# A linear-attention and MLP block on one core: tile 3 of x loaded ahead of the keys' weight, tile 0 worked in halves, and the orders and banks laid out anew

## The chip, the core and the metric

The kernel runs on one core of one Trainium2 chip. The core has a matrix engine (TensorE, "PE" in the profile, its weight loads "PEld"), a vector engine (VectorE, "DVE"), a scalar engine (ScalarE, "ACT"), GpSimd ("POOL") and a sync engine ("SP") that here only issues DMA transfers. Each engine runs its own list of instructions in order and waits for others by semaphores. Matmuls write to the eight banks of PSUM, of 512 float columns each; everything else lies in SBUF. The metric is the device time of one execution in microseconds, the median over several runs.

## What is computed

One transformer block in bfloat16: x has 2048 rows of 512; there are 32 heads of 16, and the MLP is 1792 wide.

```python
def _A_ref(x, wqkv, wo):                       # linear attention
    q, k, v = split(x @ wqkv)
    phi = lambda t: jnp.where(t > 0, t + 1, jnp.exp(t)) + 1e-6
    pq, pk = phi(q), phi(k)
    kv = jnp.einsum("bhsd,bhse->bhde", pk, v)
    z = jnp.einsum("bhsd->bhd", pk)
    o = (pq @ kv) / (pq @ z + 1e-6)
    return o @ wo
...
h = x + _A_ref(_layernorm(x), A_wqkv, A_wo)
h2 = h + _B_ref(_layernorm(h), B_w1, B_w2)     # relu(h' @ w1) @ w2
```

The sum over all rows in kv and z splits the program: all keys come first, then the heads' matrix, and only then the rows of h.

## The kernel before

The 2048 rows are 16 tiles of 128 (t = 0 to 15) and 4 chunks of 512 (c = 0 to 3; tiles 4c to 4c + 3). Nothing is scheduled by a planner at build time: a table of words, `ORDER` (line 18), is read from left to right, and each word calls a small function (`op_` and its name, lines 181 to 563) that issues a few instructions with the numbers behind the points. So each engine's list is the table's order, filtered by engine; a word's place against words of other engines means nothing except through data. Semaphores between engines are set by the framework from what is written and read. The numbers of a word say the tile or chunk, often a PSUM bank, and a first column block and a count where the work is split.

The words that matter, with the line of their instruction:

- `lx.t.n` (219), `lk`, `lq`, `lv`, `lo`, `l1`, `l2` (225): loads of n tiles of x, and of the weights; all on SP.
- `S`, `A` (253, 254): statistics of a tile of x on DVE; `R` (259, 260): one over the standard deviation on ACT; `N` (267): the normalised tile on DVE. Small letters `s`, `a`, `r`, `n` (255, 256, 259, 275) do the same for h; `n` leaves the scale out, and `r` is applied in the last step.
- `T.t.b` (292): four transposes of a normalised tile on TensorE into bank b; `E` (302): ACT's copy of them to lnT. `X` and `x` (313, 314) do both in one DMA transpose, issued by SP; `x.t` reads hn, which `n.t` writes.
- `K.t.b.k.n` (321): n of the four key matmuls of a tile; `F`, `U`, `M`, `D` make the map phi of it. `Q` and `qF` to `qD` are the same for the queries.
- `G`, `z`, `kv`, `m`, `d4`, `wb`, `rb`, `ab`, `dm`: the heads' matrices and the denominators.
- `h.t.b` (501): attention output of a tile on TensorE, `hD` (507) the sum with x on DVE.
- `p.c.f.b` (516), `ph` (525, half the columns): block f of the MLP's first layer for chunk c, 4 matmuls that read the chunk's lnT, all 512 columns of it; `pD` (536, DVE) and `pA` (531, ACT): relu of one or two blocks.
- `f.t.b.f0.n` (545): n of the 14 matmuls of the second layer for a tile; `fo` (553): the last sum on DVE; `fd` (560): the store on SP, in full or, as `fd.t.0.2` and `fd.t.2.2`, in halves of 256 columns.

```python
def op_p(c, f, b):
    for kd in range(KD):
        nc.tensor.matmul(bk[:, b, :], lhsT=w1_sb[:, kd, f * P : (f + 1) * P], rhs=lnT[c][:, kd, :], ...)
op_x = lambda t: nc.sync.dma_start_transpose(out=lnT_of(t), in_=hn[:, t % NQ, :])
op_fd = lambda t, k=0, w=KD: store(nc.sync, t, k, w)
```

The buffers lnT of chunks 0 to 3 are used twice, first for x's rows, then for h's. hn holds eight tiles, o_t (named gT in the profile) four. SP issues its transfers strictly in the table's order: a transfer whose data are not ready holds up all behind it.

Of the kernel before, what the change touches and what calls it, by code (L numbers as in the profile page):

```python
# [15 lines left out]


ORDER = """
table const lx.0.1 warm.66.7.64 lx.1.1 masks lx.2.1 lk.0.4 lx.3.1 S.0 lx.4.2 S.1 lx.6.2 lq.0.4 A.0 A.1 S.2 R.0.1
warm.2.7 lx.8.4 R.1.1 N.0 lx.12.4 A.2 N.1 T.0.1 R.2.1 T.1.6 E.0 N.2 E.1 T.2.4 S.3 K.0.2 E.2 A.3 S.4 K.1.4.2.2 R.3.1  # L20
K.1.4.0.2 F.0.1 N.3 A.4 U.0.1 S.5 T.3.5 K.2.6.2.2 E.3 S.7 K.2.6.0.2 F.1.1 K.3.3.0.2 M.0.1 A.5 U.1.1 D.0.1 K.3.3.2.2
M.1.1 R.4.2 Q.0.3.1 S.6 F.3.1 A.7 A.6 N.5 F.2.1 Q.0.1.5 N.4 X.5 R.6.2 D.1.1 T.4.7 U.3.1 M.2.1 Q.0.0.4 M.3.1 S.8 E.4
lo.0.2 U.2.1 S.10 Q.0.2.0 qF.0.0.2 N.6 K.4.2 N.7 X.6 A.10 A.8 qU.0.0.2 S.9 K.5.3 D.3.1 X.7 A.9 D.2.1 R.8.2 G.0 S.15
F.4.2 N.8 G.1 S.13 X.8 U.4.2 S.14 G.3 qU.0.2.2 A.13 S.12 lv.0.2 G.2 M.4.2 A.12 N.9 K.7.3 R.12.2 A.15 D.4.2 X.9
qF.0.2.2 K.6.2 N.12 A.14 S.11 R.14.2 X.12 K.8.0 F.6.2 N.15 N.14 G.4 A.11 N.13 U.6.2 M.6.2 X.13 qM.0.0.2 K.9.1 R.10.2
qD.0.0.2 K.12.2 X.15 D.6.2 U.8.2 za.4.1 G.5 F.8.2 X.14 K.13.3 N.11 N.10 za.6.0 G.6 X.11 U.12.2 G.7 M.8.2 F.12.2 X.10
qM.0.2.2 K.14.0 D.8.2 M.12.2 K.15.1 lv.2.2 za.8.0 l1.0.2 K.11.3 l1.2.2 F.14.2 D.12.2 K.10.2 zf U.14.2 qD.0.2.2 G.9 zhi
F.10.2 M.14.2 G.13 zlo U.10.2 G.8 M.10.2 D.14.2 G.12 D.10.2 z.0.0 z.2.0 z.3.0 z.1.0 G.15 zc zh d4.0.2 G.11 dl4.0 dx4.0
G.14 wb.0 G.10 lo.2.2 Q.1.1.1 gA.2.2 gD.0.2 rb.0.4 Q.1.0.0 ab.0.1 rb.0.6 ab.0.3 kv.1.7 rb.0.2 kv.3.7 ab.0.7 kv.0.7
rb.0.0 kv.2.7 ab.0.5 Q.1.3.3 l2.7.7 kx qF.1.0.2 Q.1.2.2 qU.1.0.2 qM.1.0.2 m.0.4 m.2.6 m.1.5 qF.1.2.2 qD.1.0.2 m.3.7  # L30
Q.2.0.0 mD.0.2 mA.2.2 Q.2.1.1 qU.1.2.2 dm.0.0.2 Q.2.3.7 dm.0.2.2 qF.2.0.2 h.1.6 qM.1.2.2 qD.1.2.2 qU.2.0.2 h.0.2 hD.1
d4.1.4 s.1 Q.3.1.5 a.1 hD.0 nA.1 h.3.0 s.0 dl4.1 x.1 h.2.2 a.0 hD.3 nA.0 Q.2.2.6 s.3 dx4.1 x.0 Q.3.2.0 a.3 hD.2
qF.2.2.2 n.3 wb.1 Q.3.3.1 s.2 qU.2.2.2 x.3 Q.3.0.4 a.2 n.2 qF.3.2.2 qM.2.0.2 x.2 qM.2.2.2 ph.0.3.3.0 qU.3.2.2 qD.2.2.2
ph.0.0.6.0 ph.0.1.7.0 qM.3.2.2 rb.1.7 qU.3.0.2 ph.0.2.2.0 qD.3.2.2 rb.1.3 ph.0.11.1.0 rb.1.5 qD.2.0.2 ph.0.10.0.0
qF.3.0.2 rb.1.6 ph.0.10.0.1 rb.1.1 ph.0.11.1.1 rb.1.0 p.0.5.4 pD.0.10.2 rb.1.4 rb.1.2 ph.0.2.2.1 ph.0.3.3.1 l2.0.7
qM.3.0.2 ph.0.0.6.1 pD.0.2.2 p.0.6.0 ph.0.1.7.1 qD.3.0.2 p.0.4.3 pD.0.0.2 p.0.7.1 pA.0.4.2 dm.1.2.2 d4.2.5.2 dm.1.0.2
p.0.8.2 dl4.2 pD.0.6.2 dl4.3 p.0.9.3 dx4.2 p.0.13.5 dx4.3 pD.0.8.2 wb.2 r.0.4 h.4.7 h.6.0 hD.4 rb.2.3 f.3.1.0.7 rb.2.1
s.4 rb.2.0 a.4 rb.2.6 rb.2.2 p.0.12.4 rb.2.5 rb.2.7 h.7.2 pD.0.12.2 rb.2.4 f.3.1.7.7 wb.3 hD.7 s.7 h.5.4 hD.6
f.2.3.7.7 hD.5 f.1.6.0.7 dm.2.2.2 dm.2.0.2 s.6 rb.3.2 h.8.0 rb.3.7 a.6 s.5 f.1.6.7.7 rb.3.0 hD.8 rb.3.5 rb.3.6 n.4 s.8
rb.3.3 f.2.3.0.7 a.5 rb.3.1 fo.1 rb.3.4 n.5 a.7 x.5 h.9.7 n.7 n.6 fo.2 f.0.0.7.7 x.4 fo.3 dm.3.2.2 h.10.5 x.7 dm.3.0.2  # L40
h.11.6 hD.9 x.6 hD.10 h.13.3 s.10 h.15.2 fd.3.0.2 fd.3.2.2 a.10 a.8 n.10 hD.11 h.14.7 x.10 s.11 f.0.0.0.7 n.8 a.11
hD.15 s.9 p.1.3.5 hD.13 p.1.8.2 hD.14 fo.0 p.1.2.4 s.15 h.12.1 s.14 p.1.9.3 s.13 a.13 p.1.7.7 pD.1.8.2 p.1.6.6 a.9
n.11 r.8.4 n.13 p.1.12.0 n.9 r.4.4 a.14 a.15 x.9 n.14 p.1.11.3 hD.12 pD.1.2.2 p.1.13.1 x.11 p.1.10.2 n.15 pD.1.6.2 x.8
p.1.0.5 pD.1.10.2 p.1.5.4 fd.1.0.2 fd.1.2.2 x.14 p.1.1.6 s.12 pD.1.12.2 f.5.2.7.7 fd.2.0.2 fd.2.2.2 fd.0.0.2 fd.0.2.2
x.15 pD.1.0.2 p.1.4.3 p.2.2.5 pD.1.4.2 f.5.2.0.7 p.2.6.3 fo.5 p.2.7.4 p.2.3.6 pD.2.6.2 p.2.10.1 a.12 n.12 r.12.4
p.2.4.4 pD.2.2.2 x.12 f.7.0.0.7 fd.5.0.2 fd.5.2.2 x.13 f.7.0.7.7 p.2.5.5 fo.7 p.2.11.2 pD.2.4.2 p.2.12.3 pD.2.10.2
p.2.13.4 f.4.6.0.7 pD.2.12.2 p.2.0.5 p.3.2.1 p.3.3.2 f.4.6.7.7 f.6.0.0.7 fo.4 pD.3.2.2 p.3.9.7 p.3.8.6 f.6.0.7.7
pD.3.8.2 p.2.9.1 fo.6 p.2.1.6 fd.6 p.3.1.3 p.3.0.2 p.2.8.0 pD.3.0.2 p.3.11.4 pD.2.0.2 p.3.10.3 pD.2.8.2 p.3.5.2
p.3.6.6 pD.3.10.2 p.3.7.7 p.3.4.1 pD.3.6.2 f.8.3.0.7 pD.3.4.2 p.3.13.7 f.10.5.0.7 p.3.12.6 f.10.5.7.7 pD.3.12.2
f.14.4.0.7 fo.10 fd.10 fd.7 f.15.1.0.14.3.1 f.15.6.0.14.0.2 fo.15.3.1 fd.15.3.1 f.14.4.7.7 fd.4 f.8.3.7.7 f.13.0.0.7  # L50
f.9.7.0.7 f.13.0.7.7 f.11.5.7.7 fo.13 fo.15.0.2 fo.14 fd.15.0.2 f.11.5.0.7 fd.13 fo.8 fd.8 f.9.7.7.7 fo.11 f.12.1.0.7
fo.9 fd.9 fd.11 f.12.1.7.7 fd.14 f.15.2.0.14.2.1 fo.12 fd.12 fo.15.2.1 ad.15.2.1
"""


# [543 lines left out]
```

## Time and profile before

| | |
|---|---|
| median of 3 runs | 168.77 us (168.57 to 169.34) |
| profiled execution | 168.48 us |
| its span (first to last instruction) | 166.8 us |
| DVE / ACT busy | 115.9 / 49.5 us |
| DMA | 16.28 MB, 98 GB/s on average |

The span is what the profile's rows cover; the execution's time has 1.7 us around it. In the rows, "L516" is a line of the kernel, "out<-in" are the tiles written and read, "xN" the number of instructions in a merged row, and a bracket tells how long the engine had been idle before and what ended that. Matmuls are pipelined, so a row's duration is longer than the distance to the next. DMA issues ("SPq") show the time that the queue spends on issuing; the time to landing is told apart.

### The profile page before, as it was taken

Reading aid. Unit: us, or ns where it says so; the run is one execution under the profiler, and the core shown is the slowest. Engines: PE = TensorE matmul, PEld = TensorE weight load, DVE = VectorE, ACT = ScalarE, POOL = GpSimd, SP = SyncE. Lnnn points to the kernel's source line nnn. Section 1 sums busy time; section 2 is a strip of 40 time slices with the busy share of each in tenths; the row PEclk is TensorE's granted clock in tenths of the full one; section 3 lists DMA queues with packets and bytes.
Section 4 is the critical chain, followed back from the end, with each engine's and each line's share of the span. In section 5 each row is a group of like instructions: output and inputs, shape, how many; then the busy total and the mean of one; then the engine's idle time right before and its main releaser. Section 6 shows DMA issues by size and latency. Waiting matters only on the chain.

```text
span 166.8 us, 2421 instructions
## 1 busy us (share of the span) xinstructions
PE 162.6 (98%) x920; PEld 79.8 (48%) x920; DVE 115.9 (69%) x215; ACT 49.5 (30%) x83; POOL 4.8 (3%) x21
## 2 busy tenths in 40 slices
...
GB/s 113 346 300 126 125 97 103 276 253 96 170 177 51 111 135 210 72 94 56 111 109 69 0 63 93 100 30 64 0 0 4 31 0 0 7 97 2 44 95 73
DMA packets 26811, 16.28 MB, mean 98 GB/s; under 512 B 16176, under 2 KB 25776, under 8 KB 26800
## 3 DMA queue, kind: packets, MB, share of 16 engines
...
q10 hardware_dynamic: 464, 0.30, 0.7%
q8 instruction: 7, 0.11, 0.3%
q14 instruction: 4, 0.03, 0.1%
...
## 4 chain that ended last, share of the span: by engine, by line
PE 94%; DVE 2%; DMA 1%; ACT 0%; issue 0%
PE bk L545 29%; PE bk L516 26%; PE bk L321 8%; PE bk L373 8%; PE bk L329 8%; PE bk L501 8%; PE bk L525 3%; DMA x_nat<-in_A_x_dram 1%; DVE st L253 1%; PE bk L445 1%; DVE gT L553 1%; PE bk L397 1%; PE bk L292 1%; PE bk L419 1%; PE bk L431 1%; DVE h_nat L267 0%
## 5 line engine op out<-in xcount | busy, mean ns | idle before, releaser
L545 PE MATMUL bk<-w_sb,at 128*128 128x512 bf16 (+2 forms) x252 | 50.9, 355 | 0.0
L516 PE MATMUL bk<-lnT,w_sb 128*128 128x512 bf16 x200 | 45.6, 379 | 0.0
L536 DVE TENSOR_SCALAR at<-bk 128x1024 bf16<-128x1024 f32 x27 | 32.4, 1220 | 13.6 <-PE bk L516 10.6
L545 PEld LDWEIGHTS <-at 128*128 128x128 bf16 x252 | 23.5, 98 | 25.2 <-DVE at L536 0.3
L516 PEld LDWEIGHTS <-w_sb 128*128 128x128 bf16 x200 | 19.5, 98 | 23.1 <-issue 0.4
L553 DVE SCALAR_TENSOR_TENSOR gT<-bk,rstd,h_nat 128x512 bf16<-128x512 f32 (+2 forms) x18 | 12.1, 688 | 22.6 <-PE bk L545 20.2
L339 ACT ACTIVATE eb<-bk 128x1024 bf16<-128x1024 f32 (+1 forms) x18 | 16.6, 930 | 3.5 <-PE bk L419 1.6
L259 ACT ACTIVATE rstd<-mv,eps 128x2 f32<-128x2 f32 (+2 forms) x14 | 4.1, 294 | 44.4 <-DVE mv L256 41.6
L342 ACT ACTIVATE rb<-bk 128x1024 bf16<-128x1024 f32 (+1 forms) x18 | 16.6, 936 | 0.9 <-PE bk L321 0.9
L501 PE MATMUL bk<-m_sb,pqs 128*128 128x512 bf16 x64 | 15.3, 379 | 0.0
L321 PE MATMUL bk<-wk_sb,lnT 128*128 128x512 bf16 x64 | 15.1, 379 | 0.0
L329 PE MATMUL bk<-lnT,wq_sb 128*128 128x512 bf16 x64 | 15.0, 379 | 0.0
L373 PE MATMUL bk<-at,h_nat 128*128 128x512 bf16 x56 | 13.2, 379 | 0.0
L253 DVE BATCH_NORM_STATS2 st<-x_nat 128x6 f32<-128x512 bf16 x16 | 10.5, 675 | 1.9 <-DMA x_nat<-in_A_x_dram 1.9
L507 DVE TENSOR_TENSOR h_nat<-bk,x_nat 128x512 bf16<-128x512 f32 x16 | 10.7, 679 | 0.9 <-PE bk L501 0.8
L255 DVE BATCH_NORM_STATS2 st<-h_nat 128x6 f32<-128x512 bf16 x16 | 10.8, 687 | 0.2
L501 PEld LDWEIGHTS <-pqs 128*128 128x128 bf16 x64 | 6.3, 98 | 7.6
L373 PEld LDWEIGHTS <-h_nat 128*128 128x128 bf16 x64 | 6.1, 98 | 7.3 <-issue 0.2
L321 PEld LDWEIGHTS <-lnT 128*128 128x128 bf16 x64 | 6.0, 97 | 7.4 <-ACT lnT L302 0.3
L329 PEld LDWEIGHTS <-wq_sb 128*128 128x128 bf16 x64 | 6.1, 98 | 7.1 <-issue 0.2
L346 DVE TENSOR_SCALAR eb<-eb 128x1024 bf16<-128x1024 bf16 (+1 forms) x18 | 6.7, 389 | 0.3 <-ACT eb L339 0.3
L267 DVE TENSOR_SCALAR h_nat<-x_nat,mv,rstd 128x512 bf16<-128x512 bf16 x16 | 6.1, 400 | 0.3 <-ACT rstd L260 0.3
...
## 6 DMA issues: line engine op xcount, KB each, us to landing
...
x_nat<-in_A_x_dram SPq DMA_DIRECT2D x2, 512.0 KB, 7.1
...
wk_sb<-in_A_wqkv_dram SPq DMA_DIRECT2D x1, 512.0 KB, 4.2
...
```

What stands on the lines that cost most here:

```text
L253: op_S = lambda t: nc.vector.bn_stats(out=st[:, t, :], in_=x_nat[:, t, :])
L255: op_s = lambda t: nc.vector.bn_stats(out=st2[:, t, :], in_=h_nat[:, t, :])
L321: nc.tensor.matmul(bk[:, b, :], lhsT=lnT[c][:, kd, j * P : (j + 1) * P], rhs=wk_sb[:, kd, :], **part(("k", t), KD),)
L329: nc.tensor.matmul(bk[:, b, :], lhsT=wq_sb[:, kd, j * P : (j + 1) * P], rhs=lnT[c][:, kd, :], start=(kd == 0), stop=(kd == KD - 1),)
L339: nc.scalar.activation(out=buf(eb, kind, i, n), in_=bank(at_bank[kind, i], n), func=ACT.Exp)
L342: nc.scalar.activation(out=buf(rb, kind, i, n), in_=bank(at_bank[kind, i], n), func=ACT.Relu)
L373: nc.tensor.matmul(bk[:, KD + kd, :], lhsT=ln_nat[:, t, kd * P : (kd + 1) * P], rhs=pk(t)[:, 0, :], start=(not stated), stop=(len(stated) ...
L501: nc.tensor.matmul(bk[:, b, :], lhsT=pqs[:, (c * KD + jb) % NQ, j * P : (j + 1) * P], rhs=m_sb[:, jb, :], start=(jb == 0), stop=(jb == KD ...
L516: nc.tensor.matmul(bk[:, b, :], lhsT=w1_sb[:, kd, f * P : (f + 1) * P], rhs=lnT[c][:, kd, :], start=(kd == 0), stop=(kd == KD - 1),)
L536: nc.vector.tensor_scalar(out=acts[c % 2][:, f : f + n, :], in0=bank(at_bank["p", c, f], n), scalar1=-1.0, scalar2=0.0, op0=ALU.mult, op1= ...
L545: nc.tensor.matmul(bk[:, b, 0 : w * P], lhsT=acts[c % 2][:, f, j * P : (j + 1) * P], rhs=w2_sb[:, f, k * P : (k + w) * P], **part(("f", t, ...
L553: nc.vector.scalar_tensor_tensor(out=o_t[:, t % NO, cols], in0=bk[:, at_bank["f", t, k], 0 : w * P], scalar=rstd2[:, t : t + 1], in1=h_nat ...
```

## The change

Only the table changes. The first words now load tile 3 of x (`lx.3.1`) ahead of the keys' weight (`lk.0.4`). Tile 0's `N.0`, `T.0.1` and `E.0` become two each, first for columns 256 to 511, then for 0 to 255. All other words are the same in number and work, but nearly all of the table stands in a new order, with other banks. The table is a line longer, so every line of the code behind it has a number that is one higher.

```diff
-table const lx.0.1 warm.66.7.64 lx.1.1 masks lx.2.1 lk.0.4 lx.3.1 S.0 lx.4.2 S.1 lx.6.2 lq.0.4 A.0 A.1 S.2 R.0.1
-warm.2.7 lx.8.4 R.1.1 N.0 lx.12.4 A.2 N.1 T.0.1 R.2.1 T.1.6 E.0 N.2 E.1 T.2.4 S.3 K.0.2 E.2 A.3 S.4 K.1.4.2.2 R.3.1
-K.1.4.0.2 F.0.1 N.3 A.4 U.0.1 S.5 T.3.5 K.2.6.2.2 E.3 S.7 K.2.6.0.2 F.1.1 K.3.3.0.2 M.0.1 A.5 U.1.1 D.0.1 K.3.3.2.2
...
-h.11.6 hD.9 x.6 hD.10 h.13.3 s.10 h.15.2 fd.3.0.2 fd.3.2.2 a.10 a.8 n.10 hD.11 h.14.7 x.10 s.11 f.0.0.0.7 n.8 a.11
-hD.15 s.9 p.1.3.5 hD.13 p.1.8.2 hD.14 fo.0 p.1.2.4 s.15 h.12.1 s.14 p.1.9.3 s.13 a.13 p.1.7.7 pD.1.8.2 p.1.6.6 a.9
-n.11 r.8.4 n.13 p.1.12.0 n.9 r.4.4 a.14 a.15 x.9 n.14 p.1.11.3 hD.12 pD.1.2.2 p.1.13.1 x.11 p.1.10.2 n.15 pD.1.6.2 x.8
-p.1.0.5 pD.1.10.2 p.1.5.4 fd.1.0.2 fd.1.2.2 x.14 p.1.1.6 s.12 pD.1.12.2 f.5.2.7.7 fd.2.0.2 fd.2.2.2 fd.0.0.2 fd.0.2.2
-x.15 pD.1.0.2 p.1.4.3 p.2.2.5 pD.1.4.2 f.5.2.0.7 p.2.6.3 fo.5 p.2.7.4 p.2.3.6 pD.2.6.2 p.2.10.1 a.12 n.12 r.12.4
...
-fo.9 fd.9 fd.11 f.12.1.7.7 fd.14 f.15.2.0.14.2.1 fo.12 fd.12 fo.15.2.1 ad.15.2.1
+table const lx.0.1 warm.66.7.64 lx.1.1 masks lx.2.1 lx.3.1 lk.0.4 S.0 lx.4.2 S.1 lx.6.2 lq.0.4 A.0 A.1 S.2 R.0.1
+warm.2.7 lx.8.4 R.1.1 N.0.2.2 lx.12.4 A.2 N.0.0.2 T.0.2.2.2 R.2.1 N.1 T.0.6.0.2 E.0.2.2 T.1.5 N.2 E.0.0.2 S.3 E.1
+T.2.2 E.2 K.0.4 A.3 R.3.1 S.4 K.1.7.2.2 F.0.1 N.3 K.2.2.0.2 U.0.1 S.5 T.3.6 K.2.2.2.2 E.3 A.4 A.5 S.7 K.1.7.0.2 R.4.2
...
+pD.1.12.2 p.1.7.7 pD.1.8.2 p.1.1.4 a.9 p.1.4.1 a.13 a.15 pD.1.6.2 h.14.5 s.10 p.1.2.6 s.12 p.1.0.3 p.1.5.2 pD.1.0.2
+p.1.3.7 a.12 n.12 f.5.4.7.7 n.9 hD.14 x.9 a.10 n.15 pD.1.2.2 f.4.0.7.7 s.8 s.11 f.6.3.7.7 a.8 pD.1.4.2 f.4.0.0.7 n.10
+a.11 x.10 n.11 r.8.4 s.14 r.4.4 f.7.7.0.7 n.13 a.14 n.8 r.12.4 n.14 x.8 f.6.3.0.7 fd.0.0.2 fd.0.2.2 fd.1.0.2 fd.1.2.2
+fd.2.0.2 fd.2.2.2 f.5.4.0.7 x.11 f.7.7.7.7 x.13 fo.5 fd.5.0.2 fd.5.2.2 p.2.7.5 x.12 fo.7 fo.6 p.2.13.2 x.14 fo.4
...
+fo.9 fd.9 fd.14 f.15.0.0.14.2.1 fo.12 fd.12 fo.15.2.1 ad.15.2.1
```

How the lists of two engines move, at the places that the prediction speaks of. First SP at the start of the program; before:

```order
L219 DMA x_nat<-in_A_x_dram 128x512 x3
L225 DMA wk_sb<-in_A_wqkv_dram 128x4x512
L219 DMA x_nat<-in_A_x_dram 128x512
L219 DMA x_nat<-in_A_x_dram 128x1024 x2
L225 DMA wq_sb<-in_A_wqkv_dram 128x4x512
```

and now:

```order
L220 DMA x_nat<-in_A_x_dram 128x512 x4
L226 DMA wk_sb<-in_A_wqkv_dram 128x4x512
L220 DMA x_nat<-in_A_x_dram 128x1024 x2
L226 DMA wq_sb<-in_A_wqkv_dram 128x4x512
```

The fourth tile of x has gone ahead of the keys' weight wk; the rest of these rows stays.

Then SP in the MLP, where the transposed tiles of h for chunks 1 to 3 (lnT_86, lnT_87, lnT_88) and the first stores stand; before:

```order
L314 DMA_TRANSPOSE lnT_86<-hn 128x4x128 x4
L560 DMA out_dram<-gT 128x256 x2
L314 DMA_TRANSPOSE lnT_87<-hn 128x4x128 x4
L560 DMA out_dram<-gT 128x256 x2
L314 DMA_TRANSPOSE lnT_88<-hn 128x4x128
L560 DMA out_dram<-gT 128x256 x4
L314 DMA_TRANSPOSE lnT_88<-hn 128x4x128 x2
```

and now:

```order
L315 DMA_TRANSPOSE lnT_86<-hn 128x4x128 x3
L561 DMA out_dram<-gT 128x256 x2
L315 DMA_TRANSPOSE lnT_87<-hn 128x4x128 x3
L561 DMA out_dram<-gT 128x256 x6
L315 DMA_TRANSPOSE lnT_87<-hn 128x4x128
L315 DMA_TRANSPOSE lnT_88<-hn 128x4x128
L561 DMA out_dram<-gT 128x256 x2
L315 DMA_TRANSPOSE lnT_88<-hn 128x4x128 x2
```

Chunk 2's four transposes (lnT_87) stood together; now three of them, x.9, x.10 and x.8, come first, then six stores of tiles 0, 1 and 2 in halves, and x.11 behind these.

Last, DVE in the MLP, from the relu of chunk 1's first blocks to the last tiles of hn (at_101 is chunk 1's activation buffer); before:

```order
L536 TENSOR_SCALAR at_101<-bk 128x1024
L256 BN_AGGR mv_107<-st_106 128x2
L275 TENSOR_SCALAR hn<-h_nat,mv_107 128x512 x3
L256 BN_AGGR mv_107<-st_106 128x2 x2
L275 TENSOR_SCALAR hn<-h_nat,mv_107 128x512
L507 TENSOR_TENSOR h_nat<-bk,x_nat 128x512
L536 TENSOR_SCALAR at_101<-bk 128x1024
L275 TENSOR_SCALAR hn<-h_nat,mv_107 128x512
L536 TENSOR_SCALAR at_101<-bk 128x1024 x2
```

and now, from pD.1.2.2 to n.8 and n.14:

```order
L537 TENSOR_SCALAR at_101<-bk 128x1024
L256 BN_STATS st_106<-h_nat 128x6 x2
L257 BN_AGGR mv_107<-st_106 128x2
L537 TENSOR_SCALAR at_101<-bk 128x1024
L276 TENSOR_SCALAR hn<-h_nat,mv_107 128x512
L257 BN_AGGR mv_107<-st_106 128x2
L276 TENSOR_SCALAR hn<-h_nat,mv_107 128x512
L256 BN_STATS st_106<-h_nat 128x6
L276 TENSOR_SCALAR hn<-h_nat,mv_107 128x512
L257 BN_AGGR mv_107<-st_106 128x2
L276 TENSOR_SCALAR hn<-h_nat,mv_107 128x512 x2
```

Before, n.8 stood ahead of these rows, and n.11 and n.9 are among the three behind the first relu (pD.1.8.2). Now two relus (pD.1.2.2 and pD.1.4.2), three statistics and the n of tiles 10, 11 and 13 stand in these rows ahead of n.8, which is the first of the two in the last row; pD.1.0.2 and the n of tiles 12, 9 and 15 stand ahead of them.

More of the change, by code (lines that the diff above doesn't have):

```diff
@@ L18 @@
 ORDER = """
-table const lx.0.1 warm.66.7.64 lx.1.1 masks lx.2.1 lk.0.4 lx.3.1 S.0 lx.4.2 S.1 lx.6.2 lq.0.4 A.0 A.1 S.2 R.0.1
-warm.2.7 lx.8.4 R.1.1 N.0 lx.12.4 A.2 N.1 T.0.1 R.2.1 T.1.6 E.0 N.2 E.1 T.2.4 S.3 K.0.2 E.2 A.3 S.4 K.1.4.2.2 R.3.1
-K.1.4.0.2 F.0.1 N.3 A.4 U.0.1 S.5 T.3.5 K.2.6.2.2 E.3 S.7 K.2.6.0.2 F.1.1 K.3.3.0.2 M.0.1 A.5 U.1.1 D.0.1 K.3.3.2.2
-M.1.1 R.4.2 Q.0.3.1 S.6 F.3.1 A.7 A.6 N.5 F.2.1 Q.0.1.5 N.4 X.5 R.6.2 D.1.1 T.4.7 U.3.1 M.2.1 Q.0.0.4 M.3.1 S.8 E.4
-lo.0.2 U.2.1 S.10 Q.0.2.0 qF.0.0.2 N.6 K.4.2 N.7 X.6 A.10 A.8 qU.0.0.2 S.9 K.5.3 D.3.1 X.7 A.9 D.2.1 R.8.2 G.0 S.15
@@ L24 @@
[L24 to L38, printed above, removed]
@@ L39 @@
-f.2.3.7.7 hD.5 f.1.6.0.7 dm.2.2.2 dm.2.0.2 s.6 rb.3.2 h.8.0 rb.3.7 a.6 s.5 f.1.6.7.7 rb.3.0 hD.8 rb.3.5 rb.3.6 n.4 s.8
-rb.3.3 f.2.3.0.7 a.5 rb.3.1 fo.1 rb.3.4 n.5 a.7 x.5 h.9.7 n.7 n.6 fo.2 f.0.0.7.7 x.4 fo.3 dm.3.2.2 h.10.5 x.7 dm.3.0.2
-h.11.6 hD.9 x.6 hD.10 h.13.3 s.10 h.15.2 fd.3.0.2 fd.3.2.2 a.10 a.8 n.10 hD.11 h.14.7 x.10 s.11 f.0.0.0.7 n.8 a.11
-hD.15 s.9 p.1.3.5 hD.13 p.1.8.2 hD.14 fo.0 p.1.2.4 s.15 h.12.1 s.14 p.1.9.3 s.13 a.13 p.1.7.7 pD.1.8.2 p.1.6.6 a.9
-n.11 r.8.4 n.13 p.1.12.0 n.9 r.4.4 a.14 a.15 x.9 n.14 p.1.11.3 hD.12 pD.1.2.2 p.1.13.1 x.11 p.1.10.2 n.15 pD.1.6.2 x.8
@@ L44 @@
-p.1.0.5 pD.1.10.2 p.1.5.4 fd.1.0.2 fd.1.2.2 x.14 p.1.1.6 s.12 pD.1.12.2 f.5.2.7.7 fd.2.0.2 fd.2.2.2 fd.0.0.2 fd.0.2.2
-x.15 pD.1.0.2 p.1.4.3 p.2.2.5 pD.1.4.2 f.5.2.0.7 p.2.6.3 fo.5 p.2.7.4 p.2.3.6 pD.2.6.2 p.2.10.1 a.12 n.12 r.12.4
-p.2.4.4 pD.2.2.2 x.12 f.7.0.0.7 fd.5.0.2 fd.5.2.2 x.13 f.7.0.7.7 p.2.5.5 fo.7 p.2.11.2 pD.2.4.2 p.2.12.3 pD.2.10.2
-p.2.13.4 f.4.6.0.7 pD.2.12.2 p.2.0.5 p.3.2.1 p.3.3.2 f.4.6.7.7 f.6.0.0.7 fo.4 pD.3.2.2 p.3.9.7 p.3.8.6 f.6.0.7.7
-pD.3.8.2 p.2.9.1 fo.6 p.2.1.6 fd.6 p.3.1.3 p.3.0.2 p.2.8.0 pD.3.0.2 p.3.11.4 pD.2.0.2 p.3.10.3 pD.2.8.2 p.3.5.2
@@ L49 @@
-p.3.6.6 pD.3.10.2 p.3.7.7 p.3.4.1 pD.3.6.2 f.8.3.0.7 pD.3.4.2 p.3.13.7 f.10.5.0.7 p.3.12.6 f.10.5.7.7 pD.3.12.2
-f.14.4.0.7 fo.10 fd.10 fd.7 f.15.1.0.14.3.1 f.15.6.0.14.0.2 fo.15.3.1 fd.15.3.1 f.14.4.7.7 fd.4 f.8.3.7.7 f.13.0.0.7
-f.9.7.0.7 f.13.0.7.7 f.11.5.7.7 fo.13 fo.15.0.2 fo.14 fd.15.0.2 f.11.5.0.7 fd.13 fo.8 fd.8 f.9.7.7.7 fo.11 f.12.1.0.7
-fo.9 fd.9 fd.11 f.12.1.7.7 fd.14 f.15.2.0.14.2.1 fo.12 fd.12 fo.15.2.1 ad.15.2.1
+table const lx.0.1 warm.66.7.64 lx.1.1 masks lx.2.1 lx.3.1 lk.0.4 S.0 lx.4.2 S.1 lx.6.2 lq.0.4 A.0 A.1 S.2 R.0.1
@@ new lines @@
+warm.2.7 lx.8.4 R.1.1 N.0.2.2 lx.12.4 A.2 N.0.0.2 T.0.2.2.2 R.2.1 N.1 T.0.6.0.2 E.0.2.2 T.1.5 N.2 E.0.0.2 S.3 E.1
+T.2.2 E.2 K.0.4 A.3 R.3.1 S.4 K.1.7.2.2 F.0.1 N.3 K.2.2.0.2 U.0.1 S.5 T.3.6 K.2.2.2.2 E.3 A.4 A.5 S.7 K.1.7.0.2 R.4.2
+K.3.3.0.2 S.6 F.1.1 K.3.3.2.2 U.1.1 A.7 M.0.1 Q.0.2.0 A.6 M.1.1 F.2.1 D.1.1 U.2.1 Q.0.1.6 N.5 N.4 X.5 R.6.2 M.2.1
+D.0.1 T.4.7 U.3.1 Q.0.0.5 S.9 E.4 lo.0.2 N.6 F.3.1 Q.0.3.1 N.7 X.6 qU.0.0.2 S.12 K.4.2 A.9 S.8 qF.0.0.2 X.7 K.5.3
+D.2.1 A.8 M.3.1 R.8.2 S.13 G.1 F.4.2 D.3.1 S.14 G.0 U.4.2 N.9 A.13 A.14 X.9 G.3 N.8 qF.0.2.2 A.12 S.15 K.6.2 M.4.2
@@ new lines @@
+R.12.2 X.8 S.11 qU.0.2.2 K.7.3 N.12 A.11 N.13 X.12 G.2 A.15 U.6.2 qM.0.0.2 S.10 K.9.1 R.14.2 D.4.2 X.13 K.8.0 N.15
+A.10 N.14 R.10.2 X.15 qM.0.2.2 G.5 F.6.2 qD.0.0.2 N.10 G.4 F.8.2 X.14 M.6.2 N.11 K.13.3 D.6.2 U.8.2 X.10 za.4.1 K.12.2
+K.15.1 qD.0.2.2 U.12.2 X.11 M.8.2 K.14.0 za.6.0 F.12.2 l1.2.2 G.6 lv.0.2 F.14.2 M.12.2 lv.2.2 D.8.2 K.10.2 l1.0.2
+D.12.2 K.11.3 za.8.0 G.13 F.10.2 M.14.2 G.12 zf U.14.2 zhi G.7 M.10.2 U.10.2 zlo G.9 D.10.2 G.8 D.14.2 z.0.1 z.1.1
+z.2.1 z.3.1 G.15 zc zh d4.0.1 G.14 dl4.0 dx4.0 G.10 wb.0 G.11 lo.2.2 Q.1.1.2 gA.2.2 gD.0.2 rb.0.0 Q.1.0.1 ab.0.5
@@ new lines @@
+rb.0.6 ab.0.7 kv.1.5 rb.0.4 kv.0.5 ab.0.3 kv.3.5 rb.0.2 kv.2.5 ab.0.1 Q.1.2.3 l2.7.7 kx qF.1.0.2 Q.1.3.4 qU.1.0.2
+qM.1.0.2 m.1.6 m.0.5 Q.2.3.7 qF.1.2.2 mD.0.2 Q.2.0.0 qU.1.2.2 qM.1.2.2 dm.0.0.2 m.3.6 m.2.5 Q.2.1.1 dm.0.2.2 mA.2.2
+qD.1.2.2 h.1.2 qF.2.0.2 qD.1.0.2 h.0.3 hD.1 qU.2.0.2 h.3.5 s.1 a.1 hD.0 d4.1.0 nA.1 Q.2.2.6 s.0 dl4.1 x.1 h.2.3 a.0
+hD.3 nA.0 Q.3.0.4 dx4.1 hD.2 x.0 qU.2.2.2 s.3 Q.3.2.2 wb.1 a.3 qF.2.2.2 n.3 Q.3.3.3 s.2 x.3 Q.3.1.5 a.2 qF.3.2.2 n.2
+qM.2.0.2 x.2 ph.0.0.6.0 qU.3.2.2 qM.3.2.2 ph.0.1.7.0 qM.2.2.2 ph.0.10.0.0 rb.1.3 qF.3.0.2 ph.0.11.1.0 rb.1.5
@@ new lines @@
+ph.0.2.2.0 r.0.4 rb.1.7 ph.0.3.3.0 qM.3.0.2 qU.3.0.2 rb.1.0 qD.3.2.2 ph.0.11.1.1 rb.1.2 ph.0.1.7.1 qD.2.0.2 rb.1.1
+ph.0.3.3.1 qD.3.0.2 p.0.4.4 rb.1.6 qD.2.2.2 rb.1.4 p.0.5.5 l2.0.7 ph.0.10.0.1 pA.0.4.2 ph.0.0.6.1 pD.0.10.2 ph.0.2.2.1
+p.0.7.5 pD.0.2.2 p.0.6.4 dm.1.0.2 d4.2.0.2 pD.0.0.2 p.0.12.3 dl4.3 dl4.2 p.0.9.2 pD.0.6.2 dx4.2 p.0.8.1 dx4.3 wb.2
+dm.1.2.2 h.7.0 pD.0.8.2 p.0.13.4 rb.2.6 h.4.1 rb.2.0 rb.2.7 h.5.5 rb.2.1 hD.4 rb.2.3 hD.7 f.3.2.0.7 rb.2.5 s.7 rb.2.4
+wb.3 hD.5 f.1.6.0.7 rb.2.2 s.4 pD.0.12.2 h.6.1 a.7 a.4 f.3.2.7.7 hD.6 n.7 s.6 x.7 f.0.1.0.7 n.4 dm.2.2.2 dm.2.0.2
```

10 lines of the change are left out of this document (added).

## The prediction

> **What bounds the kernel now.** I read the page first, then the stretches, then the chain of waits.
>
> The page: busy shares and the chain by engine.
>
> ```profile
> span 166.8 us, 2421 instructions
> PE 162.6 (98%) x920; PEld 79.8 (48%) x920; DVE 115.9 (69%) x215; ACT 49.5 (30%) x83; POOL 4.8 (3%) x21
> PE 94%; DVE 2%; DMA 1%; ACT 0%; issue 0%
> ```
>
> The stretch table (length, busy time with count per engine, granted clock, DMA share, GB/s), for the opening and the two halves behind it:
>
> ```profile
> 5.40:6.70 1.30, 1.11 (x13) 0.91 (x12) 0.76 (x3) 1.13 (x4) 0.69 (x3) 1.00 1.14 378
> 8.60:84.00 75.40, 75.40 (x437) 36.92 (x436) 63.23 (x130) 42.94 (x65) 0.00 (x0) 1.00 0.49 141
> 84.00:164.00 80.00, 79.88 (x398) 37.60 (x396) 46.91 (x68) 1.40 (x6) 0.00 (x0) 1.00 0.18 43
> ```
>
> From 8.60 us on TensorE is never idle by more than a tenth. So nothing behind the opening can be won by a better order: an order can only keep this or put a hole in it. The number of matmuls and their shapes stay as they are. The chain shows where the matmuls start and where they end (start, duration, what):
>
> ```profile
> 5.97 0.42 DVE h_nat L267
> 6.40 0.05 issue
> 6.44 0.40 PE bk L292 x4
> 6.84 1.88 PE bk L321 x8
> 8.72 0.30 PE bk L292 x4
> ...
> 93.88 8.63 PE bk L516 x40
> ...
> 111.57 3.02 PE bk L545 x14
> ```
>
> One matmul of 512 columns takes its place for 8.63/40 = 0.216 us; the second layer's agree (3.02/14 = 0.216). Eight of them are 1.73, yet 1.88 stands at 6.84, and the four transposes of tile 3 (L292) follow at 8.72: about 0.15 us is lost there. That, and what lies between 5.4 and 6.7 (1.30 − 1.11 = 0.19 us idle), is all that the opening can give behind tile 0.
>
> **The opening.** Three edits: tile 3's load goes ahead of wk, tile 0 is normalised, transposed and copied in halves, and the orders of DVE and ACT follow.
>
> ```profile
> 2.18 0.43 SPq L225 DMA_DIRECT2D wk_sb<-in_A_wqkv_dram  x1
> 2.66 1.45 SPq L219 DMA_DIRECT2D x_nat<-in_A_x_dram  x3
> wk_sb<-in_A_wqkv_dram SPq DMA_DIRECT2D x1, 512.0 KB, 4.2
> 6.64 0.69 DVE L253 BATCH_NORM_STATS2 st<-x_nat 128x6 f32<-128x512 bf16 x1 [0.26 <-DMA x_nat<-in_A_x_dram]
> 6.07 1.57 ACT L302 ACTIVATE lnT<-bk 128x512 bf16<-128x512 bf16 x3
> 6.72 2.00 PE L321 MATMUL bk<-wk_sb,lnT 128*128 128x512 bf16 x8
> ```
>
> wk is issued at 2.18 and lands 4.2 later, at 6.38; the first key matmul stands at 6.72. Tile 3, issued behind it, lands at 6.64, where its statistics stop waiting. Exchanged, wk is issued 0.48 later (2.66 − 2.18). Bounds for its landing: 6.38, if the extra 128 KB ahead cost nothing, and 2.66 + 4.2 = 6.86, if all of the delay stays. I take 6.64, the time at which both had landed before. So the first key matmul stays near 6.7 (6.7 to 6.9): tile 0's halves cannot bring it forward, since its weight is not there.
>
> The halves cost instructions. A DVE half costs between 0.2 (half of the row at 5.97) and 0.42, an ACT half between 0.26 (half of 1.57/3) and 0.52. So at most 0.4 more on DVE and 0.5 more on ACT, and as little as nothing. Cover: ACT's copies wait for wk's landing anyway; without it the first keys would be up to 0.5 later. What is won is tile 3: its statistics lose the 0.26 us wait, so its transposes can follow the eight key matmuls directly, 0.15 us earlier. The opening in sum: −0.15, with 0.0 to 0.2 for wk; I take −0.1, from −0.3 to +0.15.
>
> **The third chunk: where a wait arises.** The first matmul of p.2 (line 516, chunk 2) reads all of lnT2, so it needs the DMA transposes of tiles 8 to 11. Before:
>
> ```profile
> 88.24 12.45 SPq L314 DMA_TRANSPOSE lnT<-hn  x4
> 100.73 1.68 SPq L560 DMA_DIRECT2D out_dram<-gT  x2
> 104.02 1.73 PE bk L516 x8
> ```
>
> The four issues end at 100.69, ahead of the stores, and p.2.2.5, the second half of the eight matmuls at 104.02, starts near 104.9. Even the slowest landing among the sixteen (3.5, row below) is there by 103.
>
> In the changed order SP issues x.9, x.10 and x.8, then six stores (tiles 0, 1, 2 in halves), and only then x.11. And n.8, for which x.8 waits, comes last but one in a row of twenty DVE instructions that begins with pD.1.0.2. That one waits for p.1.0.3 on TensorE. Call A the time at which the last matmul of p.1.0.3 gives up its place.
>
> *TensorE from A*: p.1.5.2 and p.1.3.7, 8 × 0.216 = 1.73, then eight half accumulations f of tiles 4 to 7, 56 × 0.216 = 12.08. It wants p.2.7.5 at A + 13.8.
>
> *DVE from A.* The rows (merged ones tell the pitch):
>
> ```profile
> L516 PE MATMUL bk<-lnT,w_sb 128*128 128x512 bf16 x200 | 45.6, 379 | 0.0
> 99.24 2.35 DVE L536 TENSOR_SCALAR at<-bk 128x1024 bf16<-128x1024 f32 x2
> 94.78 1.23 DVE L536 TENSOR_SCALAR at<-bk 128x1024 bf16<-128x1024 f32 x1 [0.45 <-PE bk L516]
> 92.24 1.87 DVE L255 BATCH_NORM_STATS2 st<-h_nat 128x6 f32<-128x512 bf16 x3
> 96.01 0.84 DVE L275 TENSOR_SCALAR hn<-h_nat,mv 128x512 bf16<-128x512 bf16 x3
> 96.77 0.24 DVE L256 BATCH_NORM_AGGREGATE mv<-st 128x2 f32<-128x6 f32 x2
> 110.16 0.17 DVE L256 BATCH_NORM_AGGREGATE mv<-st 128x2 f32<-128x6 f32 x1
> 110.37 0.35 DVE L275 TENSOR_SCALAR hn<-h_nat,mv 128x512 bf16<-128x512 bf16 x1
> 85.02 1.28 DVE L507 TENSOR_TENSOR h_nat<-bk,x_nat 128x512 bf16<-128x512 f32 x2
> ```
>
> A matmul's result comes 0.379 − 0.216 = 0.16 behind its place, so DVE starts at about A + 0.2. Three pD at 2.35 − 1.23 = 1.12: 3.36. Three statistics at (1.87 − 0.69)/2 = 0.59 (0.69 is one alone, as at 6.64): 1.77. Seven n at (0.84 − 0.35)/2 = 0.25: 1.72, and 0.1 for the last one's full length. Five a at 0.07 (0.24 − 0.17): 0.35; two of them are followed by the n that reads them, which costs 0.14 more each (110.37 − 110.16 = 0.21): 0.28. One hD at 0.60. Sum 8.2: n.8 is done at A + 8.4. This is DVE's own work end to end; I find only pD.1.2.2 waiting for TensorE, and p.1.3.7 is done at A + 1.9, before DVE gets to it at about A + 3. Before A DVE has slack: from p.1.7.7 to p.1.0.3 TensorE has five groups of four (4.3 us), DVE two pD, three a and two statistics (about 3.6).
>
> *SP from n.8.*
>
> ```profile
> 110.75 1.19 SPq L314 DMA_TRANSPOSE lnT<-hn  x1
> 111.99 1.04 SPq L560 DMA_DIRECT2D out_dram<-gT  x2
> 113.08 1.20 SPq L314 DMA_TRANSPOSE lnT<-hn  x1
> 103.76 2.00 SPq L560 DMA_DIRECT2D out_dram<-gT  x4
> lnT<-hn SPq DMA_TRANSPOSE x16, 2.4
> DMA to landing us min/median/max: 2.4/2.4/3.5
> ```
>
> The transpose x.8 holds SP for 1.24 (111.99 − 110.75). Each store holds it about 0.5 (2.00/4), six 3.0; their data were written long ago, so it is issue time alone. x.11 is issued at A + 8.4 + 1.24 + 3.0 = A + 12.65 and lands 2.4 later, at A + 15.05; with 0.05 until TensorE starts, A + 15.1. **The hole is 15.1 − 13.8 = 1.3 us**, and everything behind it on TensorE shifts.
>
> Bounds: DVE's sum ±0.2; six stores 2.8 to 3.5; the landing 2.4 to 3.5. So 0.9 to 3.1, with the upper end only if the slow landing hits this transpose. I take 1.3: fourteen or so of sixteen rows lie at the median.
>
> Nothing gives it back: TensorE was full from there to the end, and the end is the same in both orders (seven matmuls of tile 12, a quarter of tile 15, two adds, two stores). Elsewhere banks and order change by the hundreds; I allow ±0.2 for a copy that arrives a little late.
>
> [...]
>
> **Sum.** −0.1 + 1.3 = +1.2. The profiled execution took 168.48 (span 166.8 plus 1.7 around it), so it would be 169.7; the median of the three runs is 168.77 (168.57 to 169.34), so I forecast 168.77 + 1.2 = **170.0 us**. Its own range is 169.5 to 170.6.
>
> **Rivals.**
>
> *The hole does not open* (0.15). The mechanism is SP's issue time: were the stores issued at 0.28 or less each, x.11 would come 1.3 earlier and land in time, and only the opening would be left: 168.77 − 0.15 = 168.6, no change. For it: a store's issue alone costs nothing but SP's time, and issues differ. Against it: the shortest issue shown above is wk's 0.43, at which six would save 0.4 of the 1.3, and the stores' own rows say 0.5. An earlier n.8 would do the same, but needs 1.3 out of 8.2 us of DVE rows that hardly vary.
>
> *The slow landing hits x.11* (0.08). The largest of sixteen is 3.5, that is 1.1 more: 168.77 + 1.2 + 1.1 = 171.1. Against it: most lie at 2.4.
>
> *TensorE restarts at half clock behind the hole* (0.02). In the opening the eight transposes at 5.40 still take about twice the pitch of the four at 6.44, so TensorE came to full speed only after some 5 us; a restart of that length at half speed would cost half of it, 2.5 more: 172.5. For it: the opening does show such a state. Against it: there the engine came from rest, here from full work.
>
> ```profile
> 5.40 0.86 PE L292 MATMUL bk<-ident,h_nat 128*128 128x128 bf16 x8
> ```
>
> *Faster by over 0.5%* (0.03): 0.84 us would have to come out of an opening that has 0.19 + 0.15 us idle behind its first transpose, and a first one that half a normalisation brings forward by 0.2: 168.77 − 0.54 = 168.2 at best from there. It would take 0.3 more at the end, which I do not see: 167.9.
>
> **The numbers.** The forecast has 0.72. About 0.5% (0.84 us) is what a measurement of this kernel can tell from no change. Slower by more: 0.72 + 0.08 + 0.02, less the edge of the forecast below 169.6: 0.79. Same: the first rival and that edge: 0.17. Faster: 0.04. The range 169.2 to 171.2 holds the forecast and the slow landing; the first, third and fourth rivals, 0.20 together, stay outside.
>
> **What would show it.** In the new profile: a wait of TensorE's weight loads at the first p.2 (line 517 there, since all lines move by one) for the DMA lnT<-hn, of 0.9 to 1.6 us near 115 us; six stores between the third and the fourth transpose of chunk 2 on SP; n.8 about 8.4 us behind p.1.0.3's slot; wk as the releaser of the first key matmul; tile 3's transposes right behind eight key matmuls. It is wrong if x.11 lands before TensorE has finished the eight halves f, or if another wait of similar size appears in between.

## The result, and the profile after

The changed kernel takes 170.33 us (median of five runs, 169.98 to 170.50), the kernel before 168.57 us in the same comparison (five runs, 168.37 to 169.34). The ratio is 1.0082, with a 95% interval from 1.0060 to 1.0105: slower by 1.0 to 1.8 us. The profiled execution took 170.50 us, the slowest of the five, with a span of 168.8 us against 166.8 before.

From the page of the changed kernel, the busy shares and the chain by engine:

```profile
span 168.8 us, 2395 instructions
PE 162.1 (96%) x904; PEld 79.7 (47%) x920; DVE 115.1 (68%) x216; ACT 49.6 (29%) x84; POOL 4.7 (3%) x21
PE 85%; DVE 6%; DMA 3%; SPq 2%; issue 2%; ACT 0%
```

Sixteen matmul records are missing here (904 of 920; the weight loads are all there), so merged rows of matmuls below may count one too few. What matters is the last row: TensorE carried 94% of the chain before and carries 85% now. In its place stand DVE, DMA and SP. The nine points are not time lost: where TensorE waits, the chain runs through what it waited for, and that includes DVE and SP work done while TensorE was still busy. The chain in order of time tells where, around 100 to 117 us (pieces left out are marked, except those under 0.1 us):

```profile
100.46 1.74 PE bk L517 x8
102.26 1.11 issue
...
105.11 1.13 DVE at L537
106.24 1.19 DVE st L256 x2
...
107.52 1.11 DVE at L537
108.62 0.26 DVE hn L276
...
110.31 0.51 DVE hn L276 x2
110.82 0.94 SPq L315
111.82 0.57 SPq L561
112.44 0.42 SPq L561
112.91 0.43 SPq L561
113.38 0.43 SPq L561
113.86 0.43 SPq L561
114.33 0.43 SPq L561
114.80 2.42 DMA lnT<-hn
117.27 8.59 PE bk L517 x39
```

It reads as one sentence: matmuls, then the row of DVE instructions up to n.8, then SP with the transpose of tile 8 and six stores, then the landing of tile 11's transpose, and only then matmuls again. TensorE meanwhile, in the timeline:

```profile
103.75 12.25 PE L546 MATMUL bk<-w_sb,at 128*128 128x512 bf16 x55
117.27 4.92 PE L517 MATMUL bk<-lnT,w_sb 128*128 128x512 bf16 x22 [1.28 <-DMA lnT<-hn]
```

The 56 matmuls of the second layer begin at 103.75; at 0.216 us each, 12.08 together, they give up their place at about 115.84. The first matmul of p.2 begins at 117.27. That is 1.43 us; the bracket says 1.28, because a row ends some 0.16 behind its place.

The opening: wk's issue on SP, then its row among the DMA issues (size, time from issue to landing), then DVE and TensorE in the timeline (start, duration, what).

```profile
2.65 0.43 SPq L226 DMA_DIRECT2D wk_sb<-in_A_wqkv_dram  x1
```

```profile
wk_sb<-in_A_wqkv_dram SPq DMA_DIRECT2D x1, 512.0 KB, 4.6
```

```profile
6.32 0.69 DVE L254 BATCH_NORM_STATS2 st<-x_nat 128x6 f32<-128x512 bf16 x1
6.65 0.10 PEld L322 LDWEIGHTS <-lnT 128*128 128x128 bf16 x1
7.30 1.89 PE L322 MATMUL bk<-wk_sb,lnT 128*128 128x512 bf16 x8 [0.43 <-ACT lnT L303]
9.02 0.39 PE L293 MATMUL bk<-ident,h_nat 128*128 128x128 bf16 x4
```

wk lands at 2.65 + 4.6 = 7.25 and the first key matmul stands at 7.30 (6.72 before). The bracket names ACT's copy, but TensorE had loaded the weights of this matmul from lnT, which that copy writes, at 6.65 already, so it was there; a wait for several things is put down to the one that the profile puts last, and wk's landing fits to 0.05 us. Tile 3's statistics wait for nothing now, and its transposes follow the eight key matmuls at once: 9.02 is 1.72 behind 7.30. They stood at 8.62 before, so the opening cost 0.40 in this execution.

The rest of the two spans: a half block of p.0 waited 0.12 us near 59 us for a DMA transpose (the last section tells more of this wait). 0.40 + 0.12 + 1.43 = 1.95, against 2.0 between the spans.

### The profile page after: what moved, and what is told of

Same layout as the page of the kernel before. It is cut to its first block, busy times and chain, and to the rows that moved or that the text cites. A ratio compares the mean times of both kernels' runs of the same rounds, so it can differ in the third digit from the quotient of the medians.

```text
span 168.8 us, 2395 instructions
## 1 busy us (share of the span) xinstructions
PE 162.1 (96%) x904; PEld 79.7 (47%) x920; DVE 115.1 (68%) x216; ACT 49.6 (29%) x84; POOL 4.7 (3%) x21
## 4 chain that ended last, share of the span: by engine, by line
PE 85%; DVE 6%; DMA 3%; SPq 2%; issue 2%; ACT 0%
PE bk L517 25%; PE bk L546 21%; PE bk L322 8%; PE bk L330 8%; PE bk L502 8%; PE bk L374 8%; PE bk L526 3%; SPq L561 2%; DMA lnT<-hn 1%; DVE at L537 1%; DMA x_nat<-in_A_x_dram 1%; DVE hn L276 1%; DVE st L254 1%; DVE st L256 1%; PE bk L293 1%
## 5 line engine op out<-in xcount | busy, mean ns | idle before, releaser
L546 PE MATMUL bk<-w_sb,at 128*128 128x512 bf16 (+2 forms) x248 | 49.7, 355 | 0.2
L517 PE MATMUL bk<-lnT,w_sb 128*128 128x512 bf16 x196 | 44.8, 379 | 1.5 <-DMA lnT<-hn 1.3
L268 DVE TENSOR_SCALAR h_nat<-x_nat,mv,rstd 128x512 bf16<-128x512 bf16 (+1 forms) x17 | 6.4, 389 | 0.0
```

The costliest lines, as they stand in the source:

```text
L546: nc.tensor.matmul(bk[:, b, 0 : w * P], lhsT=acts[c % 2][:, f, j * P : (j + 1) * P], rhs=w2_sb[:, f, k * P : (k + w) * P], **part(("f", t, ...
```

## The experiments

"Hole" is the distance from the place that the last matmul ahead of p.2 gives up to the first matmul of p.2, read as above. Two groups were compared with the kernel before on one chip each: the first four kernels (168.88 us before) and the last four (168.70 us before). Between the groups only the ratios to the kernel before are like for like.

**x.11 ahead of the stores.** In the table of the changed kernel:

```diff
-... n.14 x.8 f.6.3.0.7 fd.0.0.2 fd.0.2.2 fd.1.0.2 fd.1.2.2
-fd.2.0.2 fd.2.2.2 f.5.4.0.7 x.11 f.7.7.7.7 ...
+... n.14 x.8 f.6.3.0.7 x.11 fd.0.0.2 fd.0.2.2 fd.1.0.2 fd.1.2.2
+fd.2.0.2 fd.2.2.2 f.5.4.0.7 f.7.7.7.7 ...
```

> The changed kernel with x.11 put ahead of the six stores, nothing else moved. Theory (the stores on SP make the hole): x.11 is issued 1.24 us behind x.8, near 111.8, lands near 114.3, before TensorE wants it at 115.8; the hole of 1.44 us goes to under 0.1 and the span from 168.8 to about 167.4. Rival (the late n.8 on DVE makes it by itself, through x.8): the hole stays at 1.0 or more and the span above 168.3.

The timeline of this kernel, SP's queue (the second row is x.11 alone, the last of the four):

```profile
103.91 8.82 SPq L315 DMA_TRANSPOSE lnT<-hn  x4
111.48 1.26 SPq L315 DMA_TRANSPOSE lnT<-hn  x1
112.79 2.94 SPq L561 DMA_DIRECT2D out_dram<-gT  x6
```

and TensorE:

```profile
103.41 12.25 PE L546 MATMUL bk<-w_sb,at 128*128 128x512 bf16 x55
115.50 2.75 PE L517 MATMUL bk<-lnT,w_sb 128*128 128x512 bf16 x12
```

The four transposes are issued by 112.73, and p.2 starts at 115.50 where the second layer's matmuls end (103.41 + 12.08 = 115.49): no hole. By the 2.42 us that it took in the changed kernel, x.11 lands at 113.9 here (an estimate), 1.5 us or a little more ahead of need; 2.94 of stores less that is the hole of 1.43. The span is 167.0, below the 167.4 expected, since the opening also went 0.38 better in this execution (tile 3's transposes at 8.64 instead of 9.02). The time is 168.81 us, and the ratio to the kernel before 0.9997 (0.9981 to 1.0013). Moving one word of the table takes back all of what the change cost. n.8 was as late as in the changed kernel (n.8 and n.14 stand 6.47 us behind the start of the second layer in both), so the rival falls.

**wk ahead of tile 3 again**, all else as changed:

```diff
-... lx.2.1 lx.3.1 lk.0.4 S.0 ...
+... lx.2.1 lk.0.4 lx.3.1 S.0 ...
```

> The changed kernel with the keys' weight loaded ahead of tile 3 again, as before the change; tile 0 stays in halves. Theory (the opening's 0.4 us were lost to wk's later landing): wk lands near 6.4 instead of 7.25, the first key matmul stands at 6.7 to 6.8 instead of 7.30, the span falls by 0.3 to 0.5 to about 168.4, and the hole ahead of p.2 stays at 1.3 to 1.5. Rival (the halves cost it, through ACT and DVE): the first key matmul stays at 7.2 or later and the span at 168.8.

Time 170.32 us, ratio 1.0081 (1.0056 to 1.0105), span 168.9; the hole is 1.45 (117.41 against 103.88 + 12.08). The first key matmul stands at 6.93, but tile 3's transposes at 8.93, hardly ahead of 9.02. A miss: the first keys come earlier, as the theory had it, and next to nothing is won by it, since tile 3 is then late; the 0.09 that is left is gone again where the second layer begins (103.88 against 103.75).

**Both edits** (x.11 ahead of the stores, wk ahead of tile 3):

> The changed kernel with both edits: x.11 ahead of the stores and wk ahead of tile 3. If the two causes are all there is: 168.8 less 1.44 less 0.4, span about 167.0 and a time within 0.3 of the kernel before. If other places of the new order cost too: a span above 167.5.

Time 168.66 us, ratio 0.9988 (0.9974 to 1.0002), span 166.8. Nothing else of the new order costs or wins anything that can be told. Beside the kernel with wk first and the hole, measured in the same group (1.0081), the hole's price is 0.93%, 1.6 us.

**x.11 behind four of the six stores** ("/" marks the end of a line of the table):

```diff
-... fd.0.0.2 fd.0.2.2 fd.1.0.2 fd.1.2.2 / fd.2.0.2 fd.2.2.2 f.5.4.0.7 x.11 f.7.7.7.7
+... fd.0.0.2 fd.0.2.2 fd.1.0.2 fd.1.2.2 / x.11 fd.2.0.2 fd.2.2.2 f.5.4.0.7 f.7.7.7.7
```

> The changed kernel with x.11 behind four of the six stores. Theory (each store ahead of x.11 costs its issue time of 0.47 us): the hole is 1.44 less 0.94, 0.5 us, and the span 167.9. Rival (it does not matter how many stores stand there): the hole stays at 1.4 or is gone.

The timeline of this kernel, SP's queue:

```profile
111.34 1.99 SPq L561 DMA_DIRECT2D out_dram<-gT  x4
113.38 1.19 SPq L315 DMA_TRANSPOSE lnT<-hn  x1
```

and TensorE:

```profile
103.27 12.25 PE L546 MATMUL bk<-w_sb,at 128*128 128x512 bf16 x55
115.90 2.32 PE L517 MATMUL bk<-lnT,w_sb 128*128 128x512 bf16 x10 [0.38 <-DMA lnT<-hn]
```

Four stores hold SP for 1.99, and the hole is 115.90 − 103.27 − 12.08 = 0.55. Time 169.39 us, ratio 1.0027 (1.0015 to 1.0039). With none, four and six stores ahead of x.11 the hole is 0, 0.55 and 1.43: the last two stores are 0.88, 0.44 each. The first four hold SP for 1.99 and make a hole of only 0.55, since without them x.11 lands about 1.5 ahead of need.

**n.8 earlier on DVE**, SP's order as changed:

```diff
-... n.11 r.8.4 s.14 r.4.4 f.7.7.0.7 n.13 a.14 n.8 r.12.4 n.14 x.8 ...
+... n.11 n.8 r.8.4 s.14 r.4.4 f.7.7.0.7 n.13 a.14 r.12.4 n.14 x.8 ...
```

> The changed kernel with n.8 put directly behind n.11 on DVE, so ahead of s.14, n.13 and a.14 (0.92 us by the prediction's rows); SP's order stays. Theory with both links (DVE's row, then SP's queue): n.8 is ready 0.9 earlier, but SP is then still busy with x.10, whose issue ends 0.4 ahead of where x.8 began; so x.8 and x.11 gain 0.4 and the hole goes from 1.44 to about 1.0, span about 168.0 when the opening goes as in the other kernels. Theory with DVE's row alone: the hole goes to 0.5. Rival (n.8 has no part in it, only the stores do): the hole stays at 1.4.

The timeline of this kernel, SP's queue:

```profile
103.77 7.16 SPq L315 DMA_TRANSPOSE lnT<-hn  x3
110.99 2.94 SPq L561 DMA_DIRECT2D out_dram<-gT  x6
113.97 2.50 SPq L315 DMA_TRANSPOSE lnT<-hn  x2
```

and TensorE:

```profile
103.27 12.25 PE L546 MATMUL bk<-w_sb,at 128*128 128x512 bf16 x55
116.44 1.90 PE L517 MATMUL bk<-lnT,w_sb 128*128 128x512 bf16 x8 [0.92 <-DMA lnT<-hn]
```

The second layer's 56 matmuls begin at 103.27, so the hole is 116.44 − 115.35 = 1.09. The time is 169.62 us, ratio 1.0073 (1.0040 to 1.0105; one of the eight runs took 171.95). This interval overlaps the changed kernel's, so the smaller hole is read from the trace, not from the times. n.8 passed s.14, n.13 and a.14, which take 0.94 in the changed kernel (109.28 to 110.22), and the hole lost 0.34: SP could not take x.8 before it was done with x.10, which waits for n.10. The issue of x.8, the last of the three from 103.77, ends 7.66 behind the start of the second layer (110.93), in the changed kernel 8.02 (111.77): a gain of 0.36. So DVE's row counts, but through the queue, and what it gains is cut there.

**The kernel before, with x.11 alone behind x.8, x.14 and the six stores:**

```diff
-... p.1.13.1 x.11 p.1.10.2 ...
+... p.1.13.1 p.1.10.2 ...
-... fd.2.0.2 fd.2.2.2 fd.0.0.2 fd.0.2.2 / x.15 ...
+... fd.2.0.2 fd.2.2.2 fd.0.0.2 fd.0.2.2 / x.11 x.15 ...
```

> The kernel before, with x.11 alone moved on SP from its place between x.9 and x.8 to behind the six stores of tiles 1, 2 and 0 (and behind x.14); no other engine's list changes. Theory (a transpose behind stores on SP makes TensorE wait): x.11 is issued near 104.5 in place of 98.1 and lands near 107, where TensorE wants it at 104.9; a hole of about 2.1 us ahead of p.2.2.5 (1.1 to 2.6), time about 170.9. Rival (the hole needs the rest of the new order): under 0.3 us.

The timeline of this kernel, SP's queue:

```profile
100.73 1.91 SPq L314 DMA_TRANSPOSE lnT<-hn  x1
102.69 2.01 SPq L560 DMA_DIRECT2D out_dram<-gT  x4
104.75 9.76 SPq L314 DMA_TRANSPOSE lnT<-hn  x3
```

and TensorE:

```profile
104.00 1.03 PE L516 MATMUL bk<-lnT,w_sb 128*128 128x512 bf16 x4
107.28 1.02 PE L516 MATMUL bk<-lnT,w_sb 128*128 128x512 bf16 x4 [2.25 <-DMA lnT<-hn]
```

x.11, the first of the three at 104.75, is there for TensorE at 107.28, which wanted it at 104.00 + 0.86 = 104.86: a hole of 2.42. Time 171.23 us (four runs, 170.68 to 172.86), ratio 1.0167 (1.0127 to 1.0207). One word moved in the old order makes the loss too, so it needs nothing else of the new one. Here x.11 is late by more than the stores alone: x.8 and x.14 stand ahead of it as well.

**The opening alone.** Two kernels more, both with x.11 ahead of the stores, have tile 0 whole:

```diff
-N.0.2.2 lx.12.4 A.2 N.0.0.2 T.0.2.2.2 R.2.1 N.1 T.0.6.0.2 E.0.2.2 T.1.5 N.2 E.0.0.2
+N.0 lx.12.4 A.2 T.0.6 R.2.1 N.1 E.0 T.1.5 N.2
```

With wk first:

> The changed kernel with x.11 ahead of the stores, wk ahead of tile 3, and tile 0 whole again: all of the opening's edits undone. If the halves are hidden behind the landing of wk and the loads: the same as with halves (168.66), within 0.2. If they win: 0.2 to 0.4 slower; if they cost: 0.2 to 0.4 faster.

168.66 us, ratio 1.0003 (0.9991 to 1.0014). With tile 3 first:

> The changed kernel with x.11 ahead of the stores and tile 3 ahead of wk, as the change has it, but tile 0 whole. If the halves are hidden: the same as with halves (168.81), within 0.2. Against the kernel with wk first and tile 0 whole it shows the exchange of the loads alone: 0.0 to 0.3 slower if wk's later landing counts, faster if tile 3's earlier one does.

168.86 us, ratio 1.0010 (0.9991 to 1.0029). Halves and whole were measured in different groups, so compare the ratios: with wk first 0.9988 with halves and 1.0003 whole, with tile 3 first 0.9997 and 1.0010. Both pairs read 0.13 to 0.15% (0.2 us) in favour of the halves, but the intervals overlap, so that the halves win is not shown, and neither is that they do nothing. The exchange of the loads was measured within a group: tile 3 first reads 0.07 to 0.09% slower (0.1 to 0.2 us), which the intervals do not separate either. The profiles of all ten kernels, read at wk's landing (issue plus landing time), the first key matmul and tile 3's transposes:

| loads | kernel | wk lands | first key | tile 3 transposed |
|---|---|---|---|---|
| wk first | before | 6.4 | 6.72 | 8.62 |
| wk first | wk ahead again | 6.6 | 6.93 | 8.93 |
| wk first | both edits | 6.3 | 6.85 | 8.69 |
| wk first | before, x.11 late | 6.2 | 6.83 | 8.63 |
| wk first | whole | 6.6 | 6.66 | 8.95 |
| tile 3 first | changed | 7.25 | 7.30 | 9.02 |
| tile 3 first | x.11 ahead | 6.9 | 6.92 | 8.64 |
| tile 3 first | four stores | 6.8 | 6.84 | 8.67 |
| tile 3 first | n.8 earlier | 6.7 | 6.67 | 8.47 |
| tile 3 first | whole | 6.8 | 6.79 | 8.52 |

With tile 3 first the first key matmul stands within 0.1 of wk's landing in every row, and tile 3 follows 1.7 to 1.85 behind. With wk first, wk is there 0.1 to 0.6 early, and tile 3 follows 1.8 to 2.3 behind, in three of the five rows later than in any row with tile 3 first. Both end between 8.5 and 9.0, and which is ahead changes from one execution to the next; the means are 8.76 with wk first and 8.66 with tile 3 first. With its landing after 4.6 us the changed kernel's profile is the one bad draw of its five.

## Why the prediction came out right, point by point

*The place and the size of the hole.* The forecast was that TensorE wants p.2 at 13.8 us behind the place of p.1.0.3's last matmul, and that tile 11's transpose is there at 15.1. The profile shows pD.1.0.2 on DVE and x.8 on SP:

```profile
102.22 1.22 DVE L537 TENSOR_SCALAR at<-bk 128x1024 bf16<-128x1024 f32 x1 [1.11 <-PE bk L517]
110.58 1.19 SPq L315 DMA_TRANSPOSE lnT<-hn  x1
```

The first had waited for the matmul's result, so the matmul's place ends at about 102.0. x.8 is issued at 110.58 (8.56 behind it; 8.4 was forecast), x.11 at 114.80 (4.22 later; 4.24 was forecast), it lands 2.42 later (2.4 was forecast), and TensorE starts at 117.27. The hole is 1.43 in place of 1.3; the row of DVE instructions, summed from merged rows, ran 0.16 longer than forecast, and that covers the 0.13 more. The experiments carry every link: the stores (0, 0.55 and 1.43 us with none, four and six), DVE's row (1.09 with n.8 earlier), and the place itself (the same move in the old order).

*That nothing gives it back.* Right: between the hole and the end both kernels run the same matmuls without a gap that shows (TensorE is busy for 59.00 of the 59 us from 104 to 163 before, and for 47.49 of the 47.70 from 117.3 to 165 now, where a missing record counts as idle), and the span grew by the holes' sum.

*The rivals.* The hole opened; the six stores took 2.94 together, 0.49 each, as their row before had said. The landing was an ordinary one (2.42 us, where the median of its kind is 2.4). TensorE did not fall to half clock behind the hole: the granted clock is 1.00 from 84 to 164 us, and the 39 matmuls behind the hole take 8.59 us, 0.22 each, as the 40 at 93.88 did before (8.63). So it was behind the hole of 2.42 in the kernel before with x.11 late: the four matmuls right behind it take 1.02 us, the four ahead of it 1.03, and the 20 soon after 4.48, 0.22 each. The span there is 2.5 longer than before, 169.3 against 166.8, so that hole cost about its own length. The longest hole ahead of p.2 here is that one; what a longer one costs was not tried. What the prediction read as half clock in the opening rests on the pitch of the first transposes alone (0.11 us for the first four, 0.06 for the four at 6.44); its own stretch table has the granted clock at 1.00 there.

*The opening* is the step that was off. It was to win 0.1, within −0.3 and +0.15; in the profiled execution it lost 0.40. What failed is the bound on wk's landing: 6.38 to 6.86 was worked out from one execution's 4.2 us, and landings 4.0 to 4.6 behind the issue are seen in ten. The value taken between the bounds was off too: 6.64 supposes that about half of the later issue (0.48) is made good, but in the mean of five profiles each wk lands 0.45 later with tile 3 first (6.86 against 6.40, issue plus landing). That the halves cannot bring the first key matmul forward because its weight is not there was right for the order with tile 3 first, in all five profiles. In the ratios of the times neither of its parts is told from nothing, to about 0.2 us.

*The sum.* 170.0 was forecast from 168.77, +1.2; measured is +1.76 between the medians, 1.0 to 1.8 by the interval. With the hole at 1.43 and the opening at zero to 0.4 this closes. That the time came within 0.33 of the forecast is in part luck: the loss was 0.56 more than forecast, and the kernel before read 168.57 in this comparison, 0.20 below the 168.77 that was started from.
